# Attention with pooled keys and a gated feed-forward: another order of the opening's steps, late queries in four transfers, three dummy products

## The chip, the cores and the metric

The kernel runs on one core of one Trainium2 chip. The metric is the device time of one execution in microseconds (us), as the median of several runs; lower is better. The profile is of one execution on the chip, recorded by the hardware profiler. In it PE is TensorE's matrix products, PEld its weight loads, DVE is VectorE, ACT is ScalarE, POOL is GpSimd and SP is SyncE. L12 is line 12 of the kernel.

## The reference

```python
B, N, C = 4, 384 * 32, 128        # queries; kv is (4, 384, 32, 128)
kv_pool = kv.reshape(B, H // 4, 4, W // 4, 4, C).mean(axis=(2, 4))
kv_flat = kv_pool.reshape(B, -1, C) @ w_sr          # 768 keys of 128 a batch
k = v = kv_flat
s = (q @ k.transpose(0, 2, 1)) / np.sqrt(C)
a = softmax(s)
x = (a @ v).reshape(B * N, C)                       # 49152 rows
out = (np.maximum(x @ w_gate, 0) * (x @ w_val)) @ w_out     # d_ff = 1536
```

Keys are means of 4x4 pixels, projected by `w_sr`; values are the same numbers as the keys. Each query row attends to the 768 keys of its batch, and the result goes through a gated feed-forward of width 1536.

## The kernel before

The 49152 rows are worked in 96 tiles of 512, numbered k; four tiles form a group. The 768 keys of a batch are six chunks of 128, numbered jc (or j in the opening). Products are taken in half precision with float sums, but for the turning and projecting of the keys of the first batch, which are in float.

A tile goes through these steps. `scores(k, jc)` (L294, L295) multiplies a chunk of keys with the turned queries `qT` into a bank and takes the exponential on ScalarE into `aT`. `values` (L305) sums exponentials times values; reciprocals and scaling are on VectorE, and a DMA transposes the result into `xT`. `value_proj(k, fb)` (L374, copied out by ScalarE at L378) and `gate_proj(k, fb)` (L385, combined by VectorE at L388) do one of twelve blocks of the feed-forward, and `out_proj` (L407) the last product.

The main loop starts at k = 4. In iteration k it takes the scores of tile k, the values of tile k-1, the feed-forward of tile k-3 and the last product of tile k-4, interleaved over twelve steps. A set `done` keeps the scores that the opening has already taken, and the loop leaves them out.

Everything before k = 4 is the opening, and its order is written out by hand as the list of words `OPENING` (L69 to L79), run by `open_step`. `ENGINES` (L65) names for some words the engine (a: ScalarE, p: GpSimd; all others VectorE), and `SUMS` (L80) says which of the four pixel lines of a chunk are added before they are turned. Chunks 0 and 1 come from the first pair of key rows, 2 and 3 from the second, 4 and 5 from the third; each pair arrives in four transfers of 512 KB, one for each line. The words:

- `a`, `b`, `c` with a chunk: an addition of two lines (L210); `p`: the addition of pixel halves.
- `T1.3`: turn and add up line 3 of chunk 1 on TensorE, four float products of 128x128 (L227); `T0.p`: the same for what `p` left, two products.
- `kvT`, `pj`, `key`: copy the turned chunk out of its bank, project it with `w_sr` (L241), keep it scaled as keys. `vt`, `val`: turn the keys into values on TensorE (L252) and keep them.
- `cast`, `qt`, `qT`: cast a query tile to half precision, turn it on TensorE with four products (L156), copy it out. For tiles 4 and 5 `qT` is a transpose by DMA from SP's queue (L163).
- `S2.0`: scores of tile 2, chunk 0. `V2.0`: tile 2's values from chunk 0, with the values as the stationary operand (L339), summed in one bank over the six chunks; `xT` copies it out.
- `U0`, `U1`, `R`: the sums of the exponentials of the first four tiles, as products with ones (L353), and their reciprocals.
- `v0.2`, `g0.2`: value and gate projection of tile 0, block 2.
- `gate22`: GpSimd reads an element of line 2 of chunk 5, and so waits for that line before it issues `W0` and `W1`, the loads of the feed-forward weights (L583, L584). `wo` loads the last weights and the queries of tiles 6 and 7.

Each engine runs its instructions in the order in which they are issued, and waits by semaphores. There are eight banks in PSUM, which all products share. Loads are issued ahead of the opening's words: key rows, `w_sr`, the queries of tiles 0 to 3 in pairs (`q_load_pair`, L127), further key rows, then the late queries of tiles 4 and 5 (`q_load_tile`, L135), all on SP's queue but for half of the first key rows. SP uses eight completion semaphores in turn, so that a transfer is issued only when the eighth before it has landed. Before the key rows arrive, TensorE multiplies `ident` with itself, `fill(4)` (L527); nobody reads the product.

Of the kernel before, what the change touches and what calls it, by code (L numbers as in the profile page):

```python
# [16 lines left out]
def kernel(  # L17
# [23 lines left out]
    nc = tc.nc  # L41
# [9 lines left out]
    T = 512  # L51
    NS = T // 128
# [10 lines left out]
    assert NFB == 2 * NJC and NST % GRP == 0 and W // r == 8 and HC == 64  # L63

    ENGINES = dict(word.split(":") for word in """  # L65
        a0:p b0:p p0:p kvT1:a key1:a val1:a a2:p kvT2:a kvT3:a kvT4:a key4:a cast0:p qT1:a
        cast2:a cast4:p cast5:p xT3:a
    """.split())
    OPENING = """  # L69
        T1.0 T1.1 cast1 a0 T1.3 b0 T1.2 kvT1 p0 cast2 pj1 T0.3 cast3 key1 cast0 T0.p kvT0 qt2 a2  # L70
        gate22 W0 W1 cast4 qT4 wo cast5 qT5 qt1 vt1 qt3 qT2 pj0 T3.0 qT1 val1 S1.1 key0 qt0 S2.0
        S2.1 T3.1 V1.1 qT3 qT0 S1.0 S0.1 vt0 b2 val0 S3.1 S0.0 T3.2 V2.1 V0.1 T3.3 kvT3 S3.0
        V1.0 pj3 c2 p2 T2.p kvT2 key3 V0.0 S1.3 vt3 pj2 S3.3 key2 val3 S2.3 V2.0 V1.3 a4 S0.3 a5
        S1.2 S3.2 S2.2 T4.2 p4 b5 T4.p vt2 V0.3 V2.3 T4.3 val2 kvT4 S0.2 c5 p5 V2.2 pj4 V1.2
        T5.p key4 kvT5 S1.4 vt4 S0.4 val4 pj5 S2.4 V0.2 V1.4 key5 S0.5 V0.4 vt5 val5 S3.4 S2.5
        V2.4 S1.5 V0.5 S3.5 U0 xT0 V1.5 v0.2 U1 xT1 R v0.4 V2.5 xT2 v0.5 v0.3 g0.2 v0.0 V3.3
        g0.4 V3.4 v0.1 V3.5 v0.6 g0.3 g0.5 v0.7 v0.10 g0.0 v0.11 g0.10 V3.2 S4.5 S4.2 g0.1 V3.0
        v0.8 S4.0 g0.6 g0.11 v0.9 g0.8 V3.1 xT3 g0.7 S4.4 g0.9
    """.split()  # L79
    SUMS = [{"a": [0, 1], "b": ["s", 2]}, {}, {"a": [0, 1], "b": ["s", 2], "c": ["s", 3]}, {}, {"a": [0, 1]}, {"a": [0, 1], "b": ["s", 2], "c": ["s", 3]}]  # L80

    const = ctx.enter_context(tc.tile_pool(name="const", bufs=1))
    work = ctx.enter_context(tc.tile_pool(name="work", bufs=2))
# [43 lines left out]
    def q_load_pair(i):  # L127
        q32 = work.tile([128, 2, NS, C], FP32, tag="q32", bufs=2, name="q32")
        nc.sync.dma_start(  # L129
            q32, q[0, i * T : (i + 2) * T, :].rearrange("(p i s) c -> p i s c", i=2, s=NS)  # L130
        )
        for n in range(2):
            q32s[i + n] = q32[:, n]

    def q_load_tile(i):  # L135
        q32 = work.tile([128, T], FP32, tag="o_t", bufs=2, name="q32_late")
        nc.sync.dma_start(
            q32, q[0, i * T : (i + 1) * T, :].rearrange("(t j s) c -> j t (s c)", j=4, s=NS)
        )
        q32s[i] = q32.rearrange("p (s c) -> p s c", s=NS)  # L140

    def q_tiles(g):
# [33 lines left out]
    def kv_load(b, pair, lines=range(r), queues=(nc.sync,)):  # L176
        if (b, pair) not in kv_in:
            kv_in[b, pair] = work.tile([128, r, 2, r, C], FP32, tag="kv_in", bufs=3, name="kv_in")
        parts = kv_in[b, pair]
        rows = kv[b, pair * 2 * HC : (pair + 1) * 2 * HC].rearrange(  # L180
            "(hp dh) (wp h dw) c -> dh hp wp (h dw c)", dh=r, h=2, dw=r
        )
        for dh in lines:
            queues[dh % len(queues)].dma_start(  # L184
                parts[:, dh].rearrange("p h dw c -> p (h dw c)"), rows[dh]
            )
# [17 lines left out]
    def line(chunk, dh):  # L204
        return kv_in[0, chunk // 2][:, dh, chunk % 2]
# [6 lines left out]
    def sum_lines(name, chunk, x, y):  # L212
        if chunk not in sums:
            sums[chunk] = work.tile([128, r, C], FP32, tag="kv_s1", bufs=2, name="kv_s1")
        add(name, sums[chunk], x, y)
# [284 lines left out]
    w_sr_f32 = const.tile([128, C], FP32)  # L500
    kv_load(0, 0, range(r), (nc.sync, nc.scalar))
    nc.sync.dma_start(w_sr_f32, w_sr)  # L502
    q_load_pair(2)
    q_load_pair(0)
    kv_load(0, 1)
    kv_load(0, 2)
    q_load_tile(4)
    q_load_tile(5)

    warm = const.tile([128, 1], FP32)  # L510
    nc.vector.memset(warm, 0.0)
# [9 lines left out]
    def fill(n):  # L521
        for _ in range(n):
            nc.tensor.matmul(
                idle, ident, ident[:, 0:1].to_broadcast([128, 512]), start=True, stop=True
            )

    fill(4)  # L527

    gate = const.tile([128, 1], FP32)
    done = set()  # L530
# [1 line left out]
    def open_step(word):  # L532
        head = "T" if word[0] == "T" else word.rstrip("0123456789.")
        at = [int(x) for x in word[len(head):].split(".") if x] if head != "T" else []
        if head in ("a", "b", "c"):
            j = at[0]
            x, y = SUMS[j][head]
            sum_lines(word, j, sums[j] if x == "s" else line(j, x), line(j, y))
# [71 lines left out]
    for k in range(LEAD, last + 1):  # L610
# [8 lines left out]
        b = k // NST + 1  # L619
        at = k % NST - (NST - NJC - 6)  # L620
        for step in range(NFB):
            kO, kF = k - LAG - 1, k - LAG
            half, i = divmod(step // 2, NJC // 2)
# [75 lines left out]
```

## Time and profile before

| | us |
|---|---|
| median of 5 runs | 1031.66 |
| lowest, highest | 1031.35, 1033.56 |
| the profiled execution | 1033.56 |
| its span, first to last instruction | 1031.8 |
| first product of the loop (L407) from the span's start | 38.59 |

The profiled execution is the highest of the five. The span is what the views below are about: times in them count from its start. The page gives each engine's busy share of the span, and the chain of work that ended last, followed back from the last instruction. The same chain can be shown piece by piece. The timeline lists instructions by their start, those of one kind next to each other merged into one row with their number; in brackets is the idle time of the engine before the row and what ended it. A last view sums up busy time and DMA traffic in chosen stretches. The granted TensorE clock is 1.00 over the whole span.

The tasks of the opening end and the loop begins within the first 39 of 1031.8 us; the other 96% of the span is the loop, which is nearly the same in both versions.

### The profile page before, as it was taken

Reading aid. Unit: us, or ns where it says so; the run is one execution under the profiler, and the core shown is the slowest. Engines: PE = TensorE matmul, PEld = TensorE weight load, DVE = VectorE, ACT = ScalarE, POOL = GpSimd, SP = SyncE. Lnnn points to the kernel's source line nnn. Section 1 sums busy time; section 2 is a strip of 40 time slices with the busy share of each in tenths; the row PEclk is TensorE's granted clock in tenths of the full one; section 3 lists DMA queues with packets and bytes.
Section 4 is the critical chain, followed back from the end, with each engine's and each line's share of the span. In section 5 each row is a group of like instructions: output and inputs, shape, how many; then the busy total and the mean of one; then the engine's idle time right before and its main releaser. Section 6 shows DMA issues by size and latency. Waiting matters only on the chain.

```text
span 1031.8 us, 19910 instructions
## 1 busy us (share of the span) xinstructions
PE 1022.9 (99%) x6508; PEld 540.7 (52%) x6508; DVE 909.7 (88%) x1666; ACT 909.5 (88%) x1742; POOL 287.9 (28%) x311
## 2 busy tenths in 40 slices
PE   8999999999999999999999999999999999999998
PEld 5455555555555555555555555555555555555555
DVE  3889898998989898998989898989898888989898
ACT  5988998888889988888888889888888898888886
POOL 3402146511211124742212121664121211111110
PEclk9999999999999999999999999999999999999999
DMA  8935396462543657926346167672653434513122
GB/s 317 114 56 82 91 190 143 75 93 41 88 66 52 75 123 159 164 58 90 51 67 86 34 85 141 142 169 58 86 75 45 72 54 65 87 32 67 32 44 50
DMA packets 327807, 93.33 MB, mean 90 GB/s; under 512 B 307480, under 2 KB 320664, under 8 KB 327704
## 3 DMA queue, kind: packets, MB, share of 16 engines
q1 hardware_dynamic: 312584, 77.97, 38.1%
q0 software_dynamic: 14688, 12.98, 11.4%
q10 hardware_dynamic: 432, 1.11, 0.4%
q8 instruction: 51, 0.84, 0.4%
q14 instruction: 52, 0.43, 0.2%
HBM read 53.94 MB, written 26.35 MB: 78 GB/s over the span
## 4 chain that ended last, share of the span: by engine, by line
PE 95%; DMA 4%; SPq 0%; POOL 0%; issue 0%; ACT 0%; ACTq 0%
PE bank_ps L385 24%; PE bank_ps L374 24%; PE bank_ps L407 23%; PE bank_ps L305 12%; PE bank_ps L294 11%; DMA q_late<-in_q_dram 1%; DMA qT<-q 1%; DMA kv_in<-in_kv_dram 1%; DMA xT<-x 1%; PE bank_ps L393 1%; PE bank_ps L259 0%; SPq L184 0%; SPq L129 0%; SPq L502 0%; POOL q L98 0%
## 5 line engine op out<-in xcount | busy, mean ns | idle before, releaser
L388 DVE SCALAR_TENSOR_TENSOR hT<-bank_ps,val 128x512 f16<-128x512 f32 x1152 | 757.7, 687 | 91.4 <-ACT val L378 70.4
L378 ACT CAST val<-bank_ps 128x512 f16<-128x512 f32 x1152 | 677.6, 589 | 103.6 <-PE bank_ps L374 101.2
L374 PE MATMUL bank_ps<-xT,wv 128*128 128x512 f16 x1152 | 436.3, 379 | 0.7 <-DMA xT<-x 0.7
L385 PE MATMUL bank_ps<-xT,wg 128*128 128x512 f16 x1152 | 436.3, 379 | 0.0
L407 PE MATMUL bank_ps<-hT,wo 128*128 128x512 f16 x1116 | 423.0, 379 | 0.0
L295 ACT ACTIVATE aT<-bank_ps 128x512 f16<-128x512 f32 x576 | 344.9, 602 | 2.2 <-PE bank_ps L294 2.2
L423 POOL TENSOR_SCALAR o_sb<-o_t 128x512 f32<-128x512 f32 x89 | 132.6, 1489 | 665.2 <-DVE rinv L313 653.0
L305 PEld LDWEIGHTS <-aT 128*128 128x128 f16 x2208 | 170.6, 98 | 130.3
L294 PE MATMUL bank_ps<-qT,kv 128*128 128x512 f16 x576 | 216.7, 379 | 0.6 <-DMA qT<-q 0.6
L305 PE MATMUL bank_ps<-kv,aT 128*128 128x129 f16 x2208 | 215.3, 220 | 0.0
L374 PEld LDWEIGHTS <-wv 128*128 128x128 f16 x1152 | 112.7, 98 | 134.1 <-DMA xT<-x 1.2
L385 PEld LDWEIGHTS <-wg 128*128 128x128 f16 x1152 | 112.7, 98 | 68.0
L407 PEld LDWEIGHTS <-wo 128*128 128x128 f16 x1116 | 109.2, 98 | 65.8
L294 PEld LDWEIGHTS <-kv 128*128 128x128 f16 x576 | 56.2, 98 | 67.7 <-DMA qT<-q 1.1
L321 DVE TENSOR_TENSOR x<-bank_ps,rinv 128x256 f16<-128x256 f32 x184 | 78.1, 425 | 6.5
L415 DVE STREAM_TRANSPOSE o_t<-bank_ps 128x512 f32<-128x512 f32 x93 | 65.7, 706 | 0.0
L114 POOL DMA_DIRECT2D q<-in_q_dram x84 | 46.2, 556 | 0.4 <-PE bank_ps L374 0.4
L194 POOL TENSOR_TENSOR s<-kv_in 128x512 f32<-128x512 f32 x36 | 44.9, 1267 | 0.0
L313 DVE RECIPROCAL rinv<-bank_ps 128x2 f32<-128x2 f32 x184 | 26.8, 146 | 0.0
L196 POOL TENSOR_TENSOR s<-s 128x512 f32<-128x512 f32 x18 | 22.8, 1267 | 1.4
L198 POOL TENSOR_TENSOR c<-s 128x256 f32<-128x256 f32 x18 | 13.1, 727 | 1.4
L421 POOL TENSOR_TENSOR o_sb<-o_t,lead_scale 128x512 f32<-128x512 f32 x4 | 4.2, 1047 | 32.2 <-DVE rinv L313 25.5
(68 smaller groups left out, 130.4 us busy)
## 6 DMA issues: line engine op xcount, KB each, us to landing
kv_in<-in_kv_dram SPq DMA_DIRECT2D x46, 512.0 KB, 6.8
out_dram<-o_sb SPq DMA_DIRECT2D x353, 64.0 KB, 2.2
q<-in_q_dram POOLq DMA_DIRECT2D x84, 128.0 KB, 4.7
xT<-x SPq DMA_TRANSPOSE x92, 2.4
out_dram<-o_sb SPq DMA_DIRECT2D x80, 16.0 KB, 1.5
placed<-blocks SPq DMA_DIRECT2D x9, 128.0 KB, 2.4
kvT<-placed SPq DMA_DIRECT2D x36, 32.0 KB, 1.8
kv_in<-in_kv_dram ACTq DMA_DIRECT2D x2, 512.0 KB, 7.8
```

What stands on the lines that cost most here:

```text
L114: nc.gpsimd.dma_start(q16[32 * j : 32 * (j + 1)].rearrange("t (i s) c -> t i s c", i=GRP), rows[j])
L294: nc.tensor.matmul(s_ps, kv16[:, k // NST, jc, 0:C], qT_of(k), start=True, stop=True)
L295: nc.scalar.activation(aTs[k][:, jc, :], s_ps, AF.Exp, scale=qk_scale)
L305: nc.tensor.matmul(x_ps[:, i, :], aTs[k][:, jc, s * 128 : (s + 1) * 128], kv16[:, k // NST, jc, C : 2 * C + 1], start=(jc == 0 and i == 0) ...
L321: nc.vector.tensor_tensor(x16s[k][:, 2 * half : 2 * half + 2, :], x_ps[:, :, 0:C], rinv.to_broadcast([128, 2, C]), op=ALU.mult,)
L374: nc.tensor.matmul(va_ps, wv16[:, fb * 128 : (fb + 1) * 128], xTs[k], start=True, stop=True)
L378: nc.scalar.copy(val, va_ps)
L385: nc.tensor.matmul(g_ps, wg16[:, fb * 128 : (fb + 1) * 128], xTs[k], start=True, stop=True)
L388: nc.vector.scalar_tensor_tensor(hTs[k][:, fb, :], g_ps, 0.0, vals.pop((k, fb)), op0=ALU.max, op1=ALU.mult)
L407: nc.tensor.matmul(o_banks[k], wo16[:, fb, :], hTs[k][:, fb, :], start=fb == 0, stop=fb == NFB - 1)
L415: nc.vector.transpose(o_t, o_banks.pop(k))
L423: nc.gpsimd.tensor_scalar(to, o_by, 1.0 / X_SCALE**2, None, op0=ALU.mult)
```

## The change

The change touches the opening alone. The words of `OPENING` stand in another order; tiles 0 to 3 are scored in full in both, but the four scores of tile 4 (`S4.5 S4.2 S4.0 S4.4`) are left out, so that the loop takes all six in k = 4. `ENGINES` gives other steps to ScalarE and GpSimd, and `SUMS` adds other lines: chunks 3 and 4 are added up in full and chunks 0 and 5 in part, where it was 2 and 5 in full and 0 and 4 in part. The number of lines turned, eleven, and of pixel sums turned, four, is the same. The first words turn line 3 of chunk 1 before lines 0 and 1. A late query tile is loaded in four transfers of 32 partitions each. The query pair of tiles 0 and 1 is loaded ahead of that of tiles 2 and 3, and tile 5 ahead of tile 4. `fill` makes three products.

```diff
     ENGINES = dict(word.split(":") for word in """
-        a0:p b0:p p0:p kvT1:a key1:a val1:a a2:p kvT2:a kvT3:a kvT4:a key4:a cast0:p qT1:a
-        cast2:a cast4:p cast5:p xT3:a
+        a0:p b0:p val0:a key1:a val1:a kvT2:a val2:a a3:p kvT3:a key3:a val3:a kvT5:a qT0:a
+        cast1:p cast2:p cast4:p cast5:p xT2:a xT3:a
     """.split())
     OPENING = """
-        T1.0 T1.1 cast1 a0 T1.3 b0 T1.2 kvT1 p0 cast2 pj1 T0.3 cast3 key1 cast0 T0.p kvT0 qt2 a2
-        gate22 W0 W1 cast4 qT4 wo cast5 qT5 qt1 vt1 qt3 qT2 pj0 T3.0 qT1 val1 S1.1 key0 qt0 S2.0
-        S2.1 T3.1 V1.1 qT3 qT0 S1.0 S0.1 vt0 b2 val0 S3.1 S0.0 T3.2 V2.1 V0.1 T3.3 kvT3 S3.0
-        V1.0 pj3 c2 p2 T2.p kvT2 key3 V0.0 S1.3 vt3 pj2 S3.3 key2 val3 S2.3 V2.0 V1.3 a4 S0.3 a5
-        S1.2 S3.2 S2.2 T4.2 p4 b5 T4.p vt2 V0.3 V2.3 T4.3 val2 kvT4 S0.2 c5 p5 V2.2 pj4 V1.2
-        T5.p key4 kvT5 S1.4 vt4 S0.4 val4 pj5 S2.4 V0.2 V1.4 key5 S0.5 V0.4 vt5 val5 S3.4 S2.5
-        V2.4 S1.5 V0.5 S3.5 U0 xT0 V1.5 v0.2 U1 xT1 R v0.4 V2.5 xT2 v0.5 v0.3 g0.2 v0.0 V3.3
-        g0.4 V3.4 v0.1 V3.5 v0.6 g0.3 g0.5 v0.7 v0.10 g0.0 v0.11 g0.10 V3.2 S4.5 S4.2 g0.1 V3.0
-        v0.8 S4.0 g0.6 g0.11 v0.9 g0.8 V3.1 xT3 g0.7 S4.4 g0.9
+        a0 cast0 T1.3 T0.3 T1.0 b0 p0 T1.1 cast1 T1.2 kvT1 qt1 T0.p kvT0 cast2 qT1 qt0 pj1 key1
+        qt2 vt1 qT0 pj0 val1 S1.1 key0 S0.1 cast3 S0.0 qT2 T2.0 vt0 val0 S2.0 qt3 a3 gate22 W0
+        W1 cast4 qT4 wo cast5 qT5 qT3 V1.1 b3 S1.0 S3.0 T2.1 S3.1 T2.2 V0.0 T2.3 kvT2 c3 S2.1
+        V3.0 p3 pj2 V3.1 key2 V1.0 T3.p kvT3 a5 S3.2 a4 p5 vt2 V0.1 pj3 V2.0 b4 key3 val2 S0.2
+        V2.1 S2.2 S0.3 S3.3 V3.2 c4 V0.2 S1.3 T5.2 T5.p T5.3 vt3 kvT5 val3 p4 S1.2 S2.3 pj5 key5
+        T4.p V1.3 kvT4 S0.5 V1.2 pj4 key4 S1.5 V0.3 vt5 val5 S0.4 V3.3 vt4 S3.4 S1.4 V0.5 val4
+        V0.4 S2.4 xT0 S3.5 V1.5 V1.4 xT1 v0.0 v0.4 g0.4 g0.0 S2.5 v0.1 U0 g0.1 v0.5 U1 R V2.4
+        v0.2 V3.5 v0.8 g0.2 v0.3 V3.4 g0.5 v0.6 V2.3 xT3 g0.3 g0.6 v0.11 v0.10 V2.2 g0.8 v0.7
+        V2.5 xT2 g0.11 g0.7 v0.9 g0.10 g0.9
     """.split()
-    SUMS = [{"a": [0, 1], "b": ["s", 2]}, {}, {"a": [0, 1], "b": ["s", 2], "c": ["s", 3]}, {}, {"a": [0, 1]}, {"a": [0, 1], "b": ["s", 2], "c": ["s", 3]}]
+    SUMS = [{"a": [0, 1], "b": ["s", 2]}, {}, {}, {"a": [0, 1], "b": ["s", 2], "c": ["s", 3]}, {"a": [0, 1], "b": ["s", 2], "c": ["s", 3]}, {"a": [0, 1]}]
...
     def q_load_tile(i):
         q32 = work.tile([128, T], FP32, tag="o_t", bufs=2, name="q32_late")
-        nc.sync.dma_start(
-            q32, q[0, i * T : (i + 1) * T, :].rearrange("(t j s) c -> j t (s c)", j=4, s=NS)
-        )
+        rows = q[0, i * T : (i + 1) * T, :].rearrange("(t j s) c -> j t (s c)", j=4, s=NS)
+        for j in range(4):
+            nc.sync.dma_start(q32[32 * j : 32 * (j + 1)], rows[j])
...
     nc.sync.dma_start(w_sr_f32, w_sr)
+    q_load_pair(0)
     q_load_pair(2)
-    q_load_pair(0)
     kv_load(0, 1)
     kv_load(0, 2)
+    q_load_tile(5)
     q_load_tile(4)
-    q_load_tile(5)
...
-    fill(4)
+    fill(3)
```

## The prediction

> **What bounds the kernel now.** I read the page's busy shares first, then the chain that ended last, then that chain piece by piece over the first 60 us, then the timeline of the opening, then busy time and traffic by stage.
>
> ```profile
> PE 1022.9 (99%) x6508; PEld 540.7 (52%) x6508; DVE 909.7 (88%) x1666; ACT 909.5 (88%) x1742; POOL 287.9 (28%) x311
> ...
> PE 95%; DMA 4%; SPq 0%; POOL 0%; issue 0%; ACT 0%; ACTq 0%
> ```
>
> TensorE is busy for the whole span, and 95% of the chain runs through it. The only other share, 4%, is DMA, and most of that lies in the opening:
>
> ```profile
> 4.49 9.08 DMA kv_in<-in_kv_dram
> 13.59 11.58 DMA q_late<-in_q_dram
> 25.23 0.62 POOL q L98
> 25.87 9.64 DMA qT<-q
> 35.55 0.61 PE bank_ps L294 x2
> ...
> 38.53 0.22 PE bank_ps L385
> 38.75 0.22 PE bank_ps L407
> ```
>
> (Start, length, what.) The chain goes kv rows, late queries (11.58 us), their cast on GpSimd, their transpose by DMA (9.64 us), and ends at 35.55 in the first scores of tile 4. From there the chain lists TensorE products at a pitch of 0.216 us. The first product of L407, at the modelled 38.75 and in the timeline at 38.59, is the first step of the loop, k=4. Loop work is the same before and after, but for four scores. So the end moves by what TensorE idles less, or more, up to that point.
>
> ```profile
> 1.35 5.74 PE L523 MATMUL bank_ps<-ident 128*128 128x512 f32 x8 [1.35 <-POOL ident masks.py:199]
> 4.08 0.34 PEld L523 LDWEIGHTS bank_ps<-ident 128*128 128x128 f32 x1 [0.52 <-issue]
> 4.93 0.34 PEld L523 LDWEIGHTS bank_ps<-ident 128*128 128x128 f32 x1 [0.52 <-issue]
> 5.63 0.19 PEld L523 LDWEIGHTS bank_ps<-ident 128*128 128x128 f32 x1 [0.37 <-issue]
> 6.07 0.19 PEld L523 LDWEIGHTS bank_ps<-ident 128*128 128x128 f32 x1 [0.24 <-issue]
> 7.00 1.09 PE L227 MATMUL bank_ps<-ident,kv_in 128*128 128x128 f32 x8
> 9.24 1.09 PE L227 MATMUL bank_ps<-ident,kv_in 128*128 128x128 f32 x8 [1.14 <-DMA kv_in<-in_kv_dram]
> ...
> 13.79 0.45 PE L241 MATMUL bank_ps<-kvT_chunk,w_sr_f 128*128 128x128 f32 x2
> ...
> 14.08 0.60 PE L227 MATMUL bank_ps<-ident,kv_in 128*128 128x128 f32 x4
> ```
>
> The four dummies are eight passes; their pitch falls from 0.85 us (4.08 to 4.93) to 0.44 (5.63 to 6.07): the clock is granted some 4.1 us after the first pass. Lines T1.0 and T1.1 run at 7.00 as their rows land, T1.3 and T1.2 at 9.24.
>
> ```profile
> 14.00:21.40 7.40, 7.40 (x50) 4.68 (x50) 4.28 (x13) 5.93 (x13) 1.37 (x2) 1.00 1.00 397
> 21.40:27.00 5.60, 5.60 (x36) 3.40 (x35) 3.63 (x10) 4.94 (x12) 4.17 (x8) 1.00 0.88 180
> 38.60:47.70 9.10, 9.10 (x44) 4.15 (x43) 8.81 (x15) 8.70 (x17) 2.37 (x5) 1.00 0.70 118
> ```
>
> (Stretch, length, busy PE, PEld, DVE, ACT, POOL, clock, DMA share, GB/s.) While kv rows come, DMA moves 397 GB/s; once only the late queries and weights are left, 180. In k=4 (last row) DVE and ACT are nearly as full as TensorE.
>
> **What the Trainium skill says.** "DMA: Bandwidth & Descriptors", section "Why a DMA increments its semaphore by 16 and not by 1": a transfer is spread over the largest number up to 16 that divides the slowest dimension of both its sides. The old late load has 4 outermost in its source, so 4 engines; each new piece has 32 on both sides, so 16. The trace agrees with the first half: 11.58 us for 256 KB, and traffic that collapses at 21.4. The new form is in no trace yet. "TensorE: Matmul & The Clock Gate", Part 1: the clock returns to half speed after an idle window of about 3.4 us, and windows run free of the program. The longest idle stretch in this trace's opening is 1.4 us, so it doesn't show that side.
>
> **Part one, the start.** Pitches come from the timeline: 0.109 us for a 128x128 float product (eight in 1.09, the last lasting 0.27), 0.164 for a first one, 0.056 for a half-precision turn, 0.216 for 512 columns, about 0.3 for a projection. Dummies are off the path: one fewer costs or saves nothing while rows are awaited. But now T1.3 stands first, and its row lands at 9.2, so T1.0 and T1.1 no longer fill 7.00 to 7.93. Five lines together run 9.24 + 0.164 + 19 x 0.109 = 11.47. Then: query pair 0 has landed (11.02, as the first pair did before), cast1 on GpSimd takes 0.87 (its row at 12.35), to 11.93, so qt1 runs to 12.21; p0, now on DVE behind cast0, takes 11.65 to 12.07, T0.p to 12.43; qt0 to 12.65; kvT1 on DVE ends 12.35, pj1 to 12.94; cast2 (pair 2 at 12.30, +0.87) releases qt2 at 13.26; key1 on ACT frees vt1 at 13.48; pj0 ends at 13.83. That is exactly the set of work (five lines, T0.p, two projections, three query turns, one value turn) that before is finished at 14.08. The bunched start is paid for by fewer waits between: 0.25 us ahead. Bounds: 0.8 late if cast, p0 and kvT1 each come a quarter later; 0.5 ahead if casts take 0.61, as the later ones do.
>
> **Part two, from there to k=4.** Work before: 28 scores, 24 lead values, 24 projections at 0.216 (16.4), six lines (2.62), three pixel turns (0.66), four projections of keys (1.25), five value turns and one query turn (0.50), the ones products (20 in 1.26, 1.27 for all): 22.7. TensorE took 38.59 - 14.08 = 24.5, so it idled 1.8: 0.8 of it for qT at 35.55, 0.4 at the four changes into and out of the ones products, the rest small waits. After: four scores less, 21.84. I walked the new order with the same durations and landings: two kv lines release SP's late-query issues at 13.59 and 14.87, and the rest follow at that pitch, 512 KB in 1.28 us, to 22.5. Engines change little: ACT gets three more small copies (0.27 each), DVE one more pixel sum (0.42). Waits that I find: S0.0 for key0 0.11; S2.0 for qT2, behind key0 and cast3 on DVE, 0.33 (queued behind S2.0 is qt3, and so qT3 and S3.0: another 0.23); pj2 for kvT2 on ACT 0.12; S0.5 and S0.4 for their keys 0.16; others 0.22; the ones changes 0.39: 1.56. Data don't bind: the last chunk needs c4 and p4 on DVE (22.5 to 23.7) and T4.p stands at 24.7. k=4 then begins at 13.83 + 21.84 + 1.56 = 37.2. Before, less the four scores (0.86), it is 37.7. Gain 0.5. The walk may err by 0.8 either way, by waits for banks above all: four lead banks are open at once from about 21 us, where before the fourth opened late.
>
> **Part three, late queries and weights.** Pieces share SP's eight completion slots and each waits for a kv line, so the last is issued at about 22.5, and lands near 25, like the first tile before (25.2): cast4, behind the weight issues on GpSimd, and qT4 (issued 25.9) don't move much. But scores of tile 4 now stand in k=4, at about 37.5, and qT4 landed at 35.5 even with the old load: the 0.8 us stall is gone either way. The weights gain, since four engines are no longer blocked: first wv halves landed at 28.4, first wg at 29.8. The new order wants them at 28.8 and 29.2; unimproved, that costs 0.6. By bytes left after 21.4 over 16 engines they come about 2 us earlier, so I take 0. wo landed 35.4, wanted at 37.2: 0. SP issues eight pieces instead of two, about 0.6 us each, but what is queued behind them there is only qT4 and qT5.
>
> **Part four, six scores in k=4.** TensorE has 42 products, 9.06 us; ACT has 18 evictions at 0.49 (four of L295 in 2.07), 8.8; so ACT hardly catches up there. DVE ends the opening some 1.5 us behind (0.61 a product, twelve of L388 in 7.35), against 38 products' worth of slack before. Cost 0 to 0.4; I take 0.1, hidden by free banks.
>
> **Sum.** -0.25 - 0.25 + 0.1 = -0.4. The profiled run took 1033.56 with span 1031.8; it was the longest of five, whose median, 1031.66, is 1.9 below it. Span 1031.4 and 1033.2 for that execution; on the median **1031.3**, range of this case 1030.6 to 1031.9.
>
> **Rivals.**
> *Waits vanish:* the walk is too strict, and all but the ones changes go: 0.25 + 1.8 - 0.4 = 1.65 gained, 1030.0. For it: hand order; against: DVE's queue in front of qT2 is plain.
> *Eviction becomes the bound:* with four lead banks open and DVE and ACT late, TensorE waits for banks from 21 us on and through k=4. Price 0.5 to 1.5 over my sum, 1032.3. For it: 8.7 to 8.8 busy of 9.1 in k=4 before; against: no bank wait in the opening before.
> *The clock drops (slower):* three dummies end at about 6.1, T1.3 comes at 9.24: 3.1 us idle, just under the window named above. If it drops, the lines run at half speed until it is regained, about 4 us as at the start: 2.0 lost, 0.8 absorbed by waits of part one, net +0.8, 1032.5; if twice as long, 4.0 lost, +2.8, 1034.5. From 2.6 us at half speed the change is slower than before. Taken: 1033.2. Against: no gap of a full window.
> *It doesn't do what it says:* the last piece, issued at 22.5, gives qT4 no earlier start. Then nothing changes in the sum, since the stall goes by the move of the scores.
>
> **How the numbers follow.** Forecast 0.5, waits vanish 0.1, eviction 0.17, clock 0.23. Below 1029.6 or above 1033.7 (0.2%, about what a measurement of this kernel can tell from no change): faster 0.02, nothing in the cases gaining over 1.7; slower 0.18, half of the clock's cases, a few of eviction's, and an unseen stall. The range for 8 in 10 takes in waits vanish and the clock's short case: 1029.9 to 1033.4.
>
> **What would show it.** L227 first at 9.2 and L241 of pj0 ending near 13.8; no wait for qT<-q at L294; L407 first at 37.2, and no dip of pitch from 0.109 to 0.22 at L227. I'm wrong if L407 starts past 38, if L227's pitch doubles, or if TensorE waits for wg, wv or banks.

## The result, and the profile after

| | before | after |
|---|---|---|
| median, us | 1031.74 (50 executions) | 1033.85 (30 executions) |
| lowest, highest | 1031.16, 1033.56 | 1031.61, 1035.03 |
| the profiled execution, its span | 1033.56, 1031.8 | 1035.03, 1033.3 |
| mean granted clock in it | 1.000 | 0.998 |
| first product of the loop (L407) | 38.59 | 38.28 |

The ratio is 1.0019, interval 1.0014 to 1.0024 (here and below from all executions, not from the two medians): 2.1 us slower where 0.4 less was forecast. The record of the granted clock begins with the first grant, at 5.48 us in before and 5.84 in after, and the mean is that of the record. Both profiled executions are the longest of their kind. The loop begins 0.3 us earlier, but with 0.86 us of scores (four at 0.216) handed to it, so what it begins with is 0.55 late even against that long execution of before.

The page of after, span, busy times and the chain's shares by engine:

```profile
span 1033.3 us, 19921 instructions
...
PE 1023.3 (99%) x6506; PEld 542.1 (52%) x6506; DVE 910.2 (88%) x1664; ACT 909.4 (88%) x1744; POOL 288.2 (28%) x311
...
PE 98%; DMA 2%; DVE 0%; ACTq 0%; ACT 0%; issue 0%
```

TensorE is now 98% of the chain, DMA 2% instead of 4%: the long road through late queries is gone from it. But PE is busy 0.4 us longer with two products fewer. More busy time for less work suggests that products have become slower somewhere. The chain of after in the opening (start, length, what):

```profile
1.41 7.41 DMA kv_in<-in_kv_dram
8.87 4.07 PE bank_ps L227 x20
...
15.09 0.98 DVE q L98
16.07 0.34 DVE qT L98
```

Twenty products of L227 take 4.07 us; at the pitch of before (0.109) it would be some 2.3. The stretches around them, cut where the trace records a change of the granted clock (length, busy PE, PEld, DVE, ACT, POOL, clock, DMA share, GB/s):

```profile
5.84:9.25 3.41, 0.95 (x5) 0.38 (x4) 0.00 (x0) 0.00 (x0) 1.26 (x1) 1.00 1.04 416
9.25:12.66 3.41, 3.41 (x18) 3.41 (x17) 1.17 (x2) 0.00 (x0) 2.75 (x3) 0.50 1.02 408
12.66:16.07 3.41, 3.23 (x29) 2.32 (x28) 2.18 (x6) 1.98 (x6) 1.27 (x1) 1.00 1.02 406
```

The clock column carries the result: full, then 0.50 for 3.41 us, then full again. In the stretch before the fall TensorE was busy 0.95 of 3.41 us. In before the stretch of 3.41 us from the first grant on is fuller, and no fall follows:

```profile
5.48:8.89 3.41, 2.61 (x12) 1.24 (x10) 0.00 (x0) 0.00 (x0) 1.27 (x1) 1.00 1.03 414
```

Half speed for 3.41 us is up to 1.7 us of lost work, and it falls on the lines T1.3 to T1.2 that everything else waits for. Of 31 executions of after with a recorded clock (one more than the table has), 24 have a mean of 0.996 to 0.998 and took 1033.2 to 1035.0 (median 1034.0); the other 7, at 0.999 or 1.000, took 1031.6 to 1033.0 (median 1032.2). Of the executions of before beside the experiments none was under 0.999.

### The profile page after: what moved, and what is told of

It is laid out like the page before. It is cut to its first block, busy times and chain, and to the rows that moved or that the text cites. A ratio compares the mean times of both kernels' runs of the same rounds, so it can differ in the third digit from the quotient of the medians.

```text
span 1033.3 us, 19921 instructions
## 1 busy us (share of the span) xinstructions
PE 1023.3 (99%) x6506; PEld 542.1 (52%) x6506; DVE 910.2 (88%) x1664; ACT 909.4 (88%) x1744; POOL 288.2 (28%) x311
## 4 chain that ended last, share of the span: by engine, by line
PE 98%; DMA 2%; DVE 0%; ACTq 0%; ACT 0%; issue 0%
PE bank_ps L374 24%; PE bank_ps L385 24%; PE bank_ps L407 23%; PE bank_ps L305 12%; PE bank_ps L294 12%; DMA xT<-x 1%; PE bank_ps L393 1%; DMA kv_in<-in_kv_dram 1%; PE bank_ps L227 1%; PE bank_ps L339 0%; PE bank_ps L259 0%; PE bank_ps L241 0%; PE bank_ps L353 0%; DVE q L98 0%; DVE qT L98 0%; PE bank_ps L156 0%
## 5 line engine op out<-in xcount | busy, mean ns | idle before, releaser
L374 PE MATMUL bank_ps<-xT,wv 128*128 128x512 f16 x1152 | 436.3, 379 | 1.3 <-DMA xT<-x 1.3
L407 PE MATMUL bank_ps<-hT,wo 128*128 128x512 f16 x1116 | 423.0, 379 | 0.0
L374 PEld LDWEIGHTS <-wv 128*128 128x128 f16 x1152 | 112.7, 98 | 134.6 <-DMA xT<-x 1.8
L407 PEld LDWEIGHTS <-wo 128*128 128x128 f16 x1116 | 109.2, 98 | 65.8
L415 DVE STREAM_TRANSPOSE o_t<-bank_ps 128x512 f32<-128x512 f32 x93 | 65.6, 706 | 0.0
```

Of the source, the lines that this page charges most:

```text
L374: nc.tensor.matmul(va_ps, wv16[:, fb * 128 : (fb + 1) * 128], xTs[k], start=True, stop=True)
L407: nc.tensor.matmul(o_banks[k], wo16[:, fb, :], hTs[k][:, fb, :], start=fb == 0, stop=fb == NFB - 1)
L415: nc.vector.transpose(o_t, o_banks.pop(k))
```

## The experiments

Two questions: what makes the clock fall, and what is left without it. All runs at a glance; a name with a_ is after with one or more edits, one with b_ is before with an edit. "k=4" is the first L407 in the profiled execution, less 0.86 where 28 scores come before it instead of 24; "xT" is a wait of L374 for xT near 434 us, counted from one start to the next less the pitch of 0.216, which is 0.16 more than the views print as idle; "end" is the time from the start of the last product to the end of the span. These three are worked out from the records of one execution each.

| kernel | median | ratio, interval | k=4 | xT | end |
|---|---|---|---|---|---|
| before | 1031.74 | | 37.72 | 0.88 | 4.05 |
| after | 1033.85 | 1.0019, 1.0014 to 1.0024 | 38.28 | 1.46 | 4.41 |
| a_fill4 | 1032.42 | 1.0007, 0.9999 to 1.0015 | 36.53 | 0 | 4.42 |
| a_fill6 | 1032.46 | 1.0007, 0.9999 to 1.0015 | 36.28 | 0.46 | 4.43 |
| a_early | 1032.20 | 1.0003, 0.9995 to 1.0011 | 36.76 | 0 | 4.43 |
| b_fill3 | 1031.76 | 1.0000, 0.9992 to 1.0009 | 36.75 | 0.93 | 3.79 |
| b_split | 1032.77 | 1.0008, 1.0000 to 1.0017 | 36.38 | 0.90 | 4.83 |
| b_noS4 | 1031.89 | 1.0002, 0.9994 to 1.0010 | 36.50 | 0.63 | 3.76 |
| a_fill4_one | 1032.68 | 1.0009, 1.0001 to 1.0017 | 37.57 | 0.87 | 3.77 |
| a_early_one | 1032.53 | 1.0009, 1.0002 to 1.0015 | 37.39 | 0 | 4.13 |
| a_fill6_one | 1032.66 | 1.0011, 1.0003 to 1.0019 | 37.25 | 1.05 | 3.76 |
| b_sp6 | 1031.30 | 0.9997, 0.9988 to 1.0005 | 36.44 | 0.30 | 4.05 |
| a_fill4_sp24 | 1032.45 | 1.0007, 1.0001 to 1.0014 | 36.72 | 0 | 4.47 |
| b_split_sp24 | 1032.48 | 1.0008, 1.0001 to 1.0015 | 36.31 | 0.72 | 4.75 |
| b_dve4 | 1032.39 | 1.0006, 0.9998 to 1.0014 | 37.75 | 0.59 | 4.21 |
| b_pool4 | 1031.85 | 1.0000, 0.9992 to 1.0008 | 36.88 | 0 | 3.82 |
| b_pool24 | 1032.04 | 1.0002, 0.9994 to 1.0011 | 37.22 | 0 | 3.48 |
| a_fill4_dve24 | 1032.19 | 1.0005, 0.9997 to 1.0013 | 36.55 | 0.34 | 3.99 |
| a_fill4_pool24 | 1031.68 | 1.0001, 0.9993 to 1.0009 | 36.88 | 0.83 | 4.10 |
| a_fill4_both24 | 1031.59 | 0.9998, 0.9989 to 1.0006 | 36.36 | 1.44 | 3.62 |

Before, run alongside, was 1031.6 to 1031.7 each time. From the first L407 to the last product, less the xT wait and less what the four scores add, every kernel takes 988.2 to 988.5: the loop is not where they differ. The xT wait scatters from 0 to 1.5 us in kernels of both kinds, so a difference of a few tenths between single traces means nothing here; how long it is in the median execution no trace shows.

**The clock: dummies or order?** a_fill4 and a_fill6 are after with more dummies:

```diff
-    fill(3)
+    fill(4)      # a_fill6: fill(6)
```

> The changed kernel with four dummy products again. Clock theory (the idle stretch between the dummies and T1.3 lets TensorE fall to half speed in most executions): the stretch shrinks from about 3.1 us to about 2.2, half-speed executions get rarer, median 0.5 to 1.5 us below the changed kernel's 1033.85, spread still wide. Order theory (the new order itself costs the time, whatever the clock): within 0.3 us of 1033.85.

> The changed kernel with six dummy products, which end near 8.6 us instead of 6.1. Clock theory: the granted clock stays 1.0 from first rise to end, spread falls to that of the kernel before (about 0.4 us), median 1031.0 to 1032.2. Order theory: median stays at 1033.5 to 1034.2.

b_fill3 is before with `fill(3)`:

> The kernel before with three dummy products, that part alone. Clock theory: T1.0 still comes at 7.0, the idle stretch is only about 1 us, clock stays 1.0, time within 0.3 us of before. If instead the number of dummies sets the clock by itself, this kernel shows half speed too and is 1 to 2 us slower.

a_early is after with its three dummies, but lines 0 and 1 of chunk 1 first again:

```diff
-        a0 cast0 T1.3 T0.3 T1.0 b0 p0 T1.1 cast1 T1.2 kvT1 qt1 ...
+        a0 cast0 T1.0 T1.1 T1.3 T0.3 b0 p0 cast1 T1.2 kvT1 qt1 ...
```

> The changed kernel, three dummies, with lines T1.0 and T1.1 turned first, as their rows land at 7.0, and T1.3 and T0.3 behind them. Clock theory: no execution shows half speed in the opening (clock 0.999 or 1.0), median 1032.0 to 1032.8, as with four or six dummies. If the number of dummies matters and not the stretch: half speed and 1033.5 to 1034.2 again.

All four kept the clock in all executions (mean at least 0.999). One dummy takes 1.4 us off the median of after, and k=4 begins 1.75 us earlier. The timeline of after (start, length, engine, line, tiles, count; in brackets the idle time before):

```profile
3.22 3.18 PE L523 MATMUL bank_ps<-ident 128*128 128x512 f32 x4
8.87 4.07 PE L227 MATMUL bank_ps<-ident,kv_in 128*128 128x128 f32 x20 [2.46 <-DMA kv_in<-in_kv_dram]
```

and of a_fill4:

```profile
3.22 4.06 PE L523 MATMUL bank_ps<-ident 128*128 128x512 f32 x6
8.78 2.40 PE L227 MATMUL bank_ps<-ident,kv_in 128*128 128x128 f32 x20 [1.50 <-DMA kv_in<-in_kv_dram]
```

The row of products comes at nearly the same time, 8.9 and 8.8; only the idle stretch ahead of it shrinks, 2.46 to 1.50, and the twenty products take 2.40 instead of 4.07. Nothing that was computed is different. The stretches of a_fill4, whose clock was first granted at 5.87, nearly as in after:

```profile
5.84:9.25 3.41, 1.91 (x8) 0.84 (x7) 0.00 (x0) 0.00 (x0) 1.27 (x2) 1.00 1.04 416
9.25:12.66 3.41, 3.07 (x32) 2.77 (x31) 1.75 (x5) 0.00 (x0) 2.74 (x3) 1.00 1.03 411
```

and the emptiest one of a_early:

```profile
7.71:11.12 3.41, 1.53 (x12) 1.29 (x12) 0.49 (x2) 0.00 (x0) 1.98 (x3) 1.00 1.04 412
```

PE busy 1.91 and 1.53 of 3.41 us kept the clock, 0.95 lost it. Of all such stretches in the twenty traces, counted from the first grant, 1.53 is the emptiest that kept it. b_fill3 shows that three dummies do no harm while T1.0 and T1.1 run at 6.80. So neither the number of dummies nor the order costs this, but both together: they leave TensorE idle for most of one whole period of the clock's record. Whether the busy share of a period decides, or the length of the idle stretch, these runs don't settle. The nearest case is a_fill4_pool24, further down: it idled 2.18 us ahead of its first L227 and kept the clock, but that stretch lies across two periods, with 1.94 and 2.40 us busy.

**Late queries in four transfers.** b_split is before with the new `q_load_tile` alone; a_fill4_one, a_early_one and a_fill6_one are after with the old single transfer, each with the edit above that keeps the clock:

```diff
-        for j in range(4):
-            nc.sync.dma_start(q32[32 * j : 32 * (j + 1)], rows[j])
+        nc.sync.dma_start(q32, rows)
```

> The kernel before with the late queries in four transfers each, that part alone. If the old load is held on four DMA engines and its 0.8 us stall before the first scores of tile 4 is real time: qT lands before 34.8 and the kernel is 0.5 to 0.8 us faster than before. If the last piece is issued so late that the transpose doesn't start earlier, or the transpose itself is what takes long: same within 0.3 us.

> The changed kernel with four dummies and the late queries in one transfer per tile. If the split costs what it cost in the old order (1.0 us): 0.5 to 1.0 below the 1032.4 of the version with four dummies and four transfers, that is 1031.4 to 1031.9, and the stretch from last product to end is 3.8 to 4.1 us instead of 4.4. If the new order itself is what is slower than before without a clock dip: 1032.4 again.

> The changed kernel with three dummies, T1.0 and T1.1 first, and late queries in one transfer per tile: what is left of the change is the order, with neither idle stretch nor split. Split theory: 1031.2 to 1031.8, stretch at the end 3.8 to 4.1. Order theory: 1032.2, as with the split.

> The changed kernel with six dummies and the late queries in one transfer per tile again. Tail theory (six further transfers in SP's instruction stream shift it so that SP is late at the last stores, and the stretch from the last product to the end of the span grows from about 3.8 to 4.1 us to 4.4 to 4.8): that stretch is at most 4.1 us again, median 1031.2 to 1031.9. Opening theory (the split costs in the opening): L407 starts earlier than the 36.3 of the version with six dummies and four transfers. Neither (the split costs this order nothing): 1032.4 again.

In the new order the split does what part three said. One of PE's waits in a_fill4_one (line, released by, us in total, times, longest):

```profile
PE bank_ps L385 <- DMA wg<-in_moe_w_gate_dram: 0.9, 1, 0.9
```

a_fill4 has no such row. a_early_one has it with 0.7, a_fill6_one with 0.4. With the single transfers k=4 begins 1.04, 0.63 and 0.97 later (in the order a_fill4, a_early, a_fill6). Yet the medians differ by 0.26, 0.33 and 0.20 only, each by itself within the scatter: the end is 4.4 us with the split and 3.8 to 4.1 without. All three kernels with single transfers stayed 0.9 to 1.0 us above before, higher than either theory of their expectations had them. In the old order, whose first `g` comes later (31.3 us in before, 28.5 in a_fill4), no wait for weights exists to be removed, and b_split, expected faster or the same, has the longer end, 4.83, and is 1.0 us above before in the median. So there is a gain at the weights, in the new order, and something at the far end of the program, a thousand microseconds later, takes most of it back.

**The four scores of tile 4.** b_noS4 is before without the words `S4.5 S4.2 S4.0 S4.4`; the loop takes all six in k=4.

> The kernel before without the four scores of tile 4 in its opening, that part alone. If most executions wait 0.8 us for qT at 35.55 as the profiled one did: 0.5 to 0.8 us faster. If that wait is of the profiled execution alone, which was the longest of its five: within 0.3 us of before.

Nothing changes (1.0002). So six scores in k=4 cost next to nothing, and removing the 0.8 us wait for qT that the profile of before shows gains nothing in the median. Of six profiled executions of the old order with old loads and the four scores, three show such a wait (before 0.6, b_dve4 1.4, b_pool4 0.5 in the waits view, which leaves out the 0.16 named above) and three none.

**The longer end.** First suspect: SP's own instructions, six more with the split. b_sp6 is before with six spare loads of 8 KB on SP; a_fill4_sp24 and b_split_sp24 have 24 of 128 bytes (here and below, the tile `spare` is allocated ahead of the loop):

```diff
+        if 60 <= k < 84:
+            nc.sync.dma_start(spare[:, k - 60 : k - 59], w_sr[0:32, k : k + 1])
```

> The kernel before with six added small loads on SP's queue, 8 KB each, which nobody reads, one in each of the loop iterations 80 to 85: SP has as many transfers as with the split late queries, and the opening is untouched. Tail theory: the stretch from the last product to the end grows to 4.4 us or more, and the time by 0.4 to 1.0 us, as with the split. Opening theory: within 0.3 us of before, stretch at most 4.1.

> The changed kernel with four dummies, and 24 added loads of 128 bytes on SP's queue, one in each of the loop iterations 60 to 83. If the longer stretch at the end comes from where SP's instructions are fetched: adding instructions moves the fetch, the stretch falls from 4.4 to 3.8 to 4.1 us and the time to 1031.8 to 1032.1. If it comes from anything else: stretch 4.4, time 1032.4 or a little more.

> The kernel before with the split and the same 24 added loads. Fetch theory: stretch at the end 3.8 to 4.1 instead of 4.8, time 1031.8 to 1032.2. If the split costs in the opening or the loop: 1032.8 again, stretch 4.8.

No move of the end by more than 0.1 us either way: this theory fell. Second suspect: with the split, VectorE and GpSimd have four instructions more each (3010 for 3006, 586 for 582 in the records of b_split and before). They are semaphore waits: GpSimd's stand at the casts of the late queries (L98), VectorE's at L415, which uses the buffers of the late queries again. In every kernel with the split, and no spare work on VectorE, an 8 KB transfer on queue 14, which the page calls "instruction", starts 0.6 to 1.3 us after the last product, and most have a second at 4.4 to 4.8. In the old order without the split the two come at 4.2 to 4.6 and 4.9 to 5.2. b_dve4 and b_pool4 are before with four spare instructions on one engine:

```diff
+        if 60 <= k < 64:
+            nc.vector.memset(spare[:, k - 60 : k - 59], 0.0)     # b_pool4: nc.gpsimd
```

> Before with four spare VectorE memsets of 32x1 in the loop (one in each of the iterations k=60 to 63), nothing else. Theory (the four instructions that the split late load adds on VectorE move a late fetch of that engine's instructions into the last stores): the 8 KB fetch on queue 14 comes under 1.5 us after the last product instead of 4.0 to 4.6, the stretch from the last product to the end grows from 3.8 to 4.1 us to 4.4 to 4.8, and the time by about 0.6, to 1032.3. Rivals (the fetch is GpSimd's, or the stretch has to do with the split transfers themselves): fetch at 4 us or later, stretch 3.8 to 4.1, time as before, 1031.7.

> Before with four spare GpSimd memsets of 32x1 in the loop (k=60 to 63), nothing else. Theory (the late fetch is VectorE's): nothing moves, fetch at 4.0 to 4.6 us after the last product, stretch 3.8 to 4.1, time 1031.7. Rival (the late fetch is GpSimd's): fetch under 1.5, stretch 4.4 to 4.8, time 1032.3.

The DMA view of 2.5 us from just before the last product. Before (queue, kind: packets, MB, share of 16 engines):

```profile
q1 hardware_dynamic: 351, 0.29, 36.7%
q10 hardware_dynamic: 144, 0.07, 9.0%
```

b_dve4:

```profile
q1 hardware_dynamic: 336, 0.26, 32.6%
q10 hardware_dynamic: 144, 0.07, 9.2%
q14 instruction: 1, 0.01, 1.6%
```

after:

```profile
q1 hardware_dynamic: 303, 0.21, 27.2%
q10 hardware_dynamic: 144, 0.07, 9.2%
q14 instruction: 1, 0.01, 2.0%
```

Four VectorE instructions alone bring a queue-14 packet to 1.33 us after the last product, as in b_split. Four of GpSimd do not; in b_pool4 the two lie at 3.80 and 5.23, where before has 4.56 and 5.18. Over all twenty traces the two packets can be told apart. One stands 0.5 us behind the end of the span where GpSimd has 582 records, within 0.02 of it where it has 586, and is gone with 24 more. The other goes with VectorE's records: 4.6 to 5.2 after the last product with 3006, 4.0 to 4.5 with 3009 (the new order alone), 1.3 with 3010, 0.6 to 0.7 with 3013 (new order and split). So each is a fetch of one engine's instructions, and its place follows from how many came before it; with the split VectorE's comes while the last stores are still landing. b_dve4's end grew less than expected (4.21, not 4.4 to 4.8), and its interval still holds 1; the median, 1032.39, is where the theory had it, 0.54 above b_pool4's.

What else moves at the end of after stands in the timeline of VectorE and the storing queues. Before:

```profile
1026.18 2.47 SPq L453 DMA_DIRECT2D out_dram<-o_sb  x3
1027.24 0.62 DVE L450 TENSOR_SCALAR o_sb<-bank_ps 128x256 f32<-128x256 f32 x2 [0.78 <-PE bank_ps L393]
```

after:

```profile
1027.32 3.04 SPq L453 DMA_DIRECT2D out_dram<-o_sb  x3
1028.73 0.62 DVE L450 TENSOR_SCALAR o_sb<-bank_ps 128x256 f32<-128x256 f32 x2 [1.13 <-PE bank_ps L393]
```

VectorE's last two copies out of the bank follow an idle 1.13 instead of 0.78, and SP's last three stores, which wait for them, take 3.04 instead of 2.47. The gap of 1.13 stands in the traces whose fetch lies at 0.6 to 0.7 and in no other. But the transfer itself doesn't make it, since the copies begin 0.12 us ahead of the last product and the transfer 0.56 behind it. And b_split, with the longest end, has 0.78; there SP is done waiting for the stores' landings 3.6 us after the last product, where it is 2.8 in before. A test is to move the fetch. a_fill4_dve24, a_fill4_pool24 and a_fill4_both24 are a_fill4 with 24 spare instructions (k=60 to 83) on VectorE, on GpSimd, on both; b_pool24 is before with GpSimd's:

> After with four dummies, and 24 spare VectorE memsets of 32x1 in the loop (k=60 to 83). Theory (VectorE's late fetch): the 8 KB fetch moves well away from the end, by some 24 instructions, the stretch from the last product to the end falls from 4.42 to 3.7 to 4.0, time falls by 0.5, from 1032.4 to about 1031.9; with the waits at the start gone as well that is no slower than before. Rivals (GpSimd's fetch, or the split itself): fetch still at 0.6, stretch 4.4, time 1032.4.

> After with four dummies, and 24 spare GpSimd memsets of 32x1 in the loop (k=60 to 83). Theory (VectorE's late fetch): nothing moves, fetch at 0.6 us after the last product, stretch 4.4, time 1032.4. Rival (GpSimd's fetch): fetch away from the end, stretch 3.7 to 4.0, time about 1031.9.

> Before with 24 spare GpSimd memsets of 32x1 in the loop (k=60 to 83). In after with four dummies the same 24 gave 1031.68 where 1032.42 had been measured without them, though VectorE's fetch stayed at 0.6 us after the last product. Theory (a fetch of GpSimd's own near the end delays the closing, and 24 instructions move it away): time falls by 0.5 here too, to 1031.2, and the stretch after the last product to 3.6. Rival (that difference was the scatter of thirteen executions, whose stretch for xT near 434 us goes from 0 to 1.5 us): time as before, 1031.7, stretch 3.8 to 4.0.

> After with four dummies and 24 spare memsets on VectorE and 24 on GpSimd in the loop. Theory (both late fetches count): stretch after the last product 3.5 to 3.7, time 1031.2, faster than before by 0.5. Rival (only VectorE's fetch counts): stretch 3.7 to 4.0, time 1031.9 to 1032.2.

With VectorE's 24 its fetch lies 7.2 us before the last product and the end is 3.99; with GpSimd's 24 VectorE's fetch stays at 0.56, and the end is 4.10 all the same; with both it is 3.62, and VectorE's copies are back at the old gap:

```profile
1026.45 0.62 DVE L450 TENSOR_SCALAR o_sb<-bank_ps 128x256 f32<-128x256 f32 x2 [0.78 <-PE bank_ps L393]
```

So the place of VectorE's fetch takes part: with it moved away, in a_fill4_dve24 and a_fill4_both24, SP is done waiting for landings 2.7 us after the last product, against 3.2 in a_fill4 and a_fill4_pool24. GpSimd's part is a different one. Among its closing instructions every trace has one idle stretch of 0.33 to 0.37 us, but for the three with 24 spare GpSimd instructions, where none is over 0.07, and whose ends are 0.3 to 0.6 shorter in both orders. Before has this stretch too, so it is no part of the difference.

The medians fall as well, 1032.42 without spare instructions, 1032.19, 1031.68, and 1031.59 with both, where 24 on SP left 1032.45; but not in step with the ends. a_fill4_dve24 has the end of before, and its median fell by 0.23 of 0.72 only; b_pool24, with the shortest end, took 1032.04, not the 1031.2 that the theory gave. Thirteen executions a kernel don't separate tenths. So the longer end is what the traces show of a_fill4's lag, 0.4 to 0.65 us; how much of that the median pays, and how a fetch that has yet to begin holds an engine up, stays open.

No version clearly beats before: b_sp6 (0.9997) and a_fill4_both24 (0.9998) have intervals that hold 1.

## Why the prediction was wrong

**Part one, the step that failed:** "Dummies are off the path: one fewer costs or saves nothing while rows are awaited." They are off the path as work, but the fourth was what kept the clock. The rival named it, with the right place, the right cause and nearly the right price at half speed (2.0 us lost, against up to 1.7 by the clock's record and 1.75 at k=4). What it took in all, 1033.2, is near 1033.85 partly by luck, since its own 0.8 of relief never came and another 0.7 us came from elsewhere. It was put at 0.23 for a reason that the runs refute, "no gap of a full window": here 2.46 us of idleness (3.1 was worked out) were followed by the fall, and 24 of 31 executions have the lower clock. The Trainium skill ("TensorE: Matmul & The Clock Gate", Part 1) speaks of at least one idle window of about 3.4 us; the trace agrees with the length, 3.41, but the window need not be empty: TensorE was busy for 0.95 of it. And its price was cut by "0.8 absorbed by waits of part one", which the runs refute too: k=4 is late by the full 1.75. pj0 ends at 14.76 in after and 13.62 in a_fill4, 1.14 of it, and the rest comes behind, as the wait of 0.4 for a qT copy on VectorE that a_fill4 doesn't have. (By the prediction's own sums, 0.8 and 0.4, the change is slower from 2.4 us at half speed on, not 2.6.) Two of its signs of being wrong came: L407 started past 38, at 38.28, and the pitch at L227 doubled. With the clock kept, part one holds: 13.62 against 13.83 forecast.

**Part two** erred twice, in opposite senses. Its walk was too strict: from pj0's end to k=4, a_fill4 takes 22.9, so 1.1 of waits for 21.84 of work where 1.56 were walked. But the base was wrong: "it idled 1.8: 0.8 of it for qT" was read from the longest execution of five and set against the median. b_noS4 shows no gain from removing this wait. Without the fall, the new order's k=4 lies at 36.3 to 36.9 in seven traces with the split; the old order's lies there in six of nine, and at 37.2 to 37.8 in three, of which two have the longest waits for qT. Old traces without such a wait, b_split and b_noS4, begin at 36.4 and 36.5, so nothing of the 0.5 is seen beyond that wait. An estimate for the median executions says the same: the median, less 1.8 outside the span (as in the profiled execution of before), less 989.1 for the loop with its four scores, less the end of the one trace, leaves for k=4 and xT together 36.7 to 37.3 in the seven, and 36.3 to 37.7 in the seven old kernels without the split.

**Part three** was right on the weights: the split takes away a wait for wg of 0.4 to 0.9 us, which at k=4 is 0.6 to 1.0, where 0.6 was worked out. The Trainium skill's reading ("DMA: Bandwidth & Descriptors", on the increment by 16) agrees with the new form in its effect: with 32 on both sides wg lands 5.1 us after issue in after, instead of 8.2 in before. On how many engines a piece ran no view here shows. What part three left out is the count of instructions: "eight pieces instead of two" was priced on SP alone, at nothing (an issue takes 0.31 us, not 0.6). The added waits on VectorE move a fetch to where the last stores are landing, and the end of the traces grew by 0.4 to 0.65 us. No rival had it.

**Part four** took 0.1; measured 0.0 to 0.3: less xT and the four scores the loop takes 988.2 in a_fill4 as in before, and 988.5 in b_noS4. No wait of PE for a bank shows in a_fill4.

**The sum** in the median: 1.43 for the clock (after to a_fill4), 0.72 for a_fill4 above its before, together 2.15 for 2.11 measured. The first is shown by one edit and by the clock of every execution. The second is less sure, as its interval (0.9999 to 1.0015) still touches 1; the traces put it at the end of the program, with what was said above left open.

## What to carry to other kernels

Work that nobody reads can hold up the clock: before taking a dummy product away, or moving the first real product behind a load, add up how busy TensorE is in each 3.4 us from the moment the clock is granted, and don't count on an idle stretch being safe because it is shorter than that: 2.46 us was not. Set a change against the executions that make the median: a wait in a profiled execution that is the longest of its kind may be that execution's own. And look at the end of the program after any edit that adds transfers or instructions, however early: four instructions at the front moved an instruction fetch to where the last stores were landing.

## What the runs showed that was not expected

- The clock fell with TensorE busy 0.95 of 3.41 us (28%), and did not with 1.53 (45%). Its record changes only at multiples of 3.413 us from the first grant; in the profiled execution of after the half speed lasts exactly one. Where between 28% and 45% the line runs, or whether a single line exists, wasn't tried.
- Seven of 31 executions of after kept the clock though nothing in the program differs. That the phase of the clock's periods decides is likely, as the first grant lies anywhere from 4.2 to 7.4 us in these traces, but wasn't tried.
- Splitting the transfer of two tiles in four each added waits on the engines that use their data or their buffers: four instructions on GpSimd and four on VectorE.
- Fetches of 8 KB of instructions arrive on queue 14 at places set by the count of instructions: four more on VectorE moved its fetch from 5.18 us after the last product to 1.33, 24 more in a_fill4 from 0.57 to 7.2 before it.
- An engine can stand idle for a third of a microsecond among its closing instructions: GpSimd did in seventeen of twenty traces, and 24 spare instructions ahead of the end took that away.
